# A new order for the first stretch of an RWKV-and-experts kernel: constant products, column turns, stores and loads around the first triangular inversion

## The chip, the cores and the metric

The kernel runs on one core of a Trainium2 chip. The metric is device time in microseconds (us): the median of several executions. One execution was also taken by the hardware profiler. All positions below are microseconds from the start of that execution's span. PE is TensorE, DVE VectorE, ACT ScalarE, POOL GpSimd; SP is the engine that here only issues DMAs.

## What is computed

A recurrence over 768 steps for 4 x 8 heads of width 40, then a dense feed-forward layer, then a layer of eight experts of which each token uses one. The change touches only the recurrence:

```python
for t in range(S):                      # S = 768
    y[:, :, t] = einsum('bhd,bhde->bhe', rt, state)
    Sa = einsum('bhde,bhe->bhd', state, at)
    state = state * wt[:, :, None, :] - einsum('bhd,bhe->bhde', Sa, bt) \
          + einsum('bhd,bhe->bhde', vt, kt)
x = y as 3072 tokens x 320
x = (h * clip(h + 3, 0, 6) / 6) @ w_out          # h = x @ w_in
out[token] = gate * relu(x @ w1[e]) @ w2[e]      # e = argmax expert of the token
```

## The kernel before

The 768 steps are cut into 24 chunks of 32. Within a chunk the recurrence becomes matrix products, for which a unit triangular 32 x 32 system per head and batch must be solved. Two neighbouring chunks are a pair. The steps, with the names that the traces show:

- A **window** is four chunks (128 partitions). `window(sc)` loads `wt`, turns and scans it (`turn`, `scan`, `carry`, `mult`), makes `Em` and its inverse `It` (`before`, `after`, `inv`), scales the rows `ra`, `rk`, `rb` by them (`scale`), and stores what later chunks need to DRAM (`keep`: `Ed`, `KBd`, `X2`, `Pd`). W0 is the first window, W1 the second. Rows 0 to 63 of a window hold its first pair, 64 to 127 its second.
- `prep_u(pair, half)` gives four units: three turn columns (`t`, PE transposes, copied out of PSUM to `Z`, `KB` or `UV`) and the fourth makes the pair's triangular matrices (`LN`, 32 products; masked to `Ns`; stored to `Nd`).
- `solve(pair)` loads `N` (and a copy `X`) from `Nd` and inverts by 30 steps of a product and a subtraction (lines L574, L575). The inverses go to `Td`, and chunks read them back as `Tb`. Pair 0 is solved on DVE, all others on POOL. Each needs its own result only at chunk 2 x pair.
- Chunk c runs, in this order on PE: `rh` (right side), `xp` (turn of the last chunk's output), `u` (product with `Tb`), `tu`, `s` (state), `g` (a triangular product, masked to `YL`), `st`, `y` (output), `vr` (columns of the next chunk). Between them stand units of `prep_u` of a later pair, pieces of the next window, weights of the dense layer (`wraw` loaded, `wf` converted in three DVE operations, `wi`, `wo`), and from chunk 2 on the products of the dense layer itself (`h`, `x`).
- `warmer(n)` and `heat(n)` issue n products of the identity with itself (`warm`), whose result nobody reads. `heat` is called at fixed places of the early chunks, and a table HEATS gives n by the number of the call.

Nothing is scheduled by a machine: each engine works through its instructions in the order in which the program writes them, and waits on semaphores. A DMA queue is in order too: an SP instruction that waits holds all behind it.

Of the kernel before, what the change touches and what calls it, by code (L numbers as in the profile page):

```python
# [42 lines left out]
def kernel(ctx, tc, r, k, v, w, a, b, w_in, w_out, mod_id, w_gate, mod_bias, w1, w2, out):  # L43
# [336 lines left out]
    def init2():  # L380
        nc.vector.tensor_copy(identr, ident)
        nc.scalar.copy(XS[:, 704:768], zeros[:, 0:64])
        nc.scalar.copy(XA[64:104].rearrange("p b h d -> p (b h) d"), ident[64:104, None, 64:104].to_broadcast([40, B * H, D]))

    def window(sc):
# [55 lines left out]
        def keep(j):  # L441

            p, c = slice(C * j, C * j + C), SC * sc + j
            nc.sync.dma_start(out=Ed[c].rearrange("b t f -> t b f"), in_=Em[p].rearrange("p b h e -> p b (h e)"))
            for x in range(2):
                if c == 0:
                    nc.sync.dma_start(out=X2[0][32 * x:32 * x + 32].rearrange("p b h e -> p (b h) e"), in_=AKB[1 + x][p, :, :, 0:D].rearrange("p b h e -> p (b h) e"))
                    continue
                nc.sync.dma_start(out=KBd[x, C * c:C * c + C].rearrange("t b (h e) -> t (b h) e", e=D), in_=AKB[1 + x][p, :, :, 0:D].rearrange("p b h e -> p (b h) e"))
            if j == 0 and sc < NSC - 1:  # L450
                nc.sync.dma_start(out=Pd[sc].rearrange("b f -> (b f)")[None, :], in_=v["I"][127:128].rearrange("p b h e -> p (b h e)"))
# [634 lines left out]
    HEATS = {2: 0, 3: 2, 5: 8, 8: 4, 9: 0, 12: 0, 14: 0, 18: 4, 20: 3, 21: 1, 24: 0, 25: 0, 26: 0, 27: 0, 29: 6, 31: 0, 32: 6, 35: 0, 37: 0, 41: 1, 43: 0, 45: 1, 47: 1, 52: 1, 53: 1, 55: 1, 61: 1, 62: 0, 64: 1, 81: 3, 82: 1, 83: 0}  # L1086
# [13 lines left out]

    def heat(n):

        n = HEATS.get(at[0], 2 if at[0] > 11 else n)
        at[0] += 1
        if n:
            warmer(n)
# [89 lines left out]
    warmer(8)  # L1196
# [3 lines left out]
    keep(0)  # L1200
    keep(1)
    WA.ahead = 0
    WA.pull(1)
    now(wq, 1)
    for kt in range(2):
        nc.sync.dma_start(out=wg[:, kt, :], in_=w_gate[128 * kt:128 * kt + 128, :])
    nc.sync.dma_start(out=wg[0:64, 2, :], in_=w_gate[256:320, :])
    loads_e(0)
    now(U[0][3])
    flush_stores()  # L1210
# [19 lines left out]
    some(2)  # L1230
    now(U[1][3])
    flush_stores()
    some(2)
    work0 = solve(0, nc.vector, None, nc.sync)
    WA.pull(2)
    keep(2)
    keep(3)
    for i in range(3):
        now(U[2][i])
        warmer(2)  # L1240
        now(U[3][i])
# [22 lines left out]
    queue.clear()  # L1264
# [16 lines left out]
    first_units = (2, 2, 1, 2, 1)  # L1281
# [4 lines left out]
    for c in range(NCH):  # L1286
        sc, j = divmod(c, SC)
        more = c + 1 < NCH
        turn = [0]
        if c == SC:  # L1290
            steady.append(True)
            M.lags = (1, 2, 4)
# [4 lines left out]
        def slot(fn, *args):  # L1297
            fn(*args)
            if hold:
                heat(dict(xpose=2, columns=2, turn_state=3, cols_vr=2).get(getattr(fn, "__name__", ""), 0) if c else 0)  # L1300
            tick()

        def dense():
            if (c, turn[0]) >= START and hold:
                hold.pop()
            if len(M.units) > RESERVE and not hold:
                M.emit(1)
            elif c < 4:
                heat(2)
                tick()  # L1310
# [50 lines left out]
        slot(rhs, c)  # L1361
        if c == 0:
            Z.append(big.tile([128, H, B, 2, C], F32, tag="Z2", name="Z2"))
            nc.scalar.copy(Z[2][0:64].rearrange("p h b j t -> p (h b j t)").rearrange("p (n x) -> p n x", x=128), zeros[0:64, None, :].to_broadcast([64, 2 * H, 128]))
            U = [prep_u(2, hf) for hf in range(2)]
            units.extend((U[0][0], U[1][0], *U[0][1:], *U[1][1:]))
# [411 lines left out]
```

## Time and profile before

| | |
|---|---|
| median of 3 runs | 1133.76 us (1129.04 to 1135.96) |
| the profiled execution's own time | 1132.62 us |
| its span | 1130.8 us |
| PE busy | 1038.7 us, 92% of the span |
| DVE, ACT, POOL busy | 675.9, 649.3, 387.5 us |
| granted TensorE clock, mean | 0.922 of full |

The first 230 us are the part in which the chunks run without much of the dense layer between them. After that PE is busy nearly all the time, with the dense layer's and the experts' products.

### The profile page before, as it was taken

The numbers are of one execution on the slowest core, as the hardware profiler recorded it, in microseconds if no ns is written. First come the engines' busy times: TensorE is split into PE (matmuls) and PEld (weight loads), VectorE is DVE, ScalarE is ACT, GpSimd is POOL, SyncE is SP. The second block draws the span as 40 slices with busy tenths as digits, with TensorE's granted clock in tenths as the row PEclk, the third lists the DMA queues.
The fourth block names the chain that finished last, engine by engine and source line by source line (L and its number), as shares of the span: only waits on it lengthen the run. The fifth ranks groups of instructions, "written<-read, shape, count | busy, mean of one in ns | idle before, by whom it ended". The sixth has DMA issues, their size and how long they took to land. (4 is left out here: it accounts for less than half of the span.)

```text
span 1130.8 us, 36970 instructions
## 1 busy us (share of the span) xinstructions
PE 1038.7 (92%) x15598; PEld 969.9 (86%) x15598; DVE 675.9 (60%) x1345; ACT 649.3 (57%) x1364; POOL 387.5 (34%) x844
## 2 busy tenths in 40 slices
PE   3967899899999999998999899999999879999995
PEld 3867898788888887887888798999999879999995
DVE  8676535755546554654335446455666897887770
ACT  4224645578777876777776673433333545666551
POOL 5326260631745738357383701000000102322221
PEclk9566957899999998999999899999999979999998
DMA  9697674997997998779756453133332757666730
GB/s 137 153 107 95 105 153 100 127 174 121 154 140 151 161 128 172 106 142 181 144 106 139 84 131 89 64 104 104 104 91 77 230 166 210 210 200 204 218 92 16
DMA packets 366265, 152.36 MB, mean 135 GB/s; under 512 B 322823, under 2 KB 348935, under 8 KB 366092
## 3 DMA queue, kind: packets, MB, share of 16 engines
q1 hardware_dynamic: 361100, 130.96, 58.9%
q0 software_dynamic: 4992, 18.96, 6.0%
q8 instruction: 125, 2.05, 0.8%
q14 instruction: 48, 0.39, 0.1%
HBM read 109.76 MB, written 40.12 MB: 133 GB/s over the span
## 5 line engine op out<-in xcount | busy, mean ns | idle before, releaser
L275 DVE SCALAR_TENSOR_TENSOR gf<-rl,h 128x512 f32<-128x512 f32 x96 | 65.7, 684 | 128.2 <-ACT rl L271 126.4
L263 PE MATMUL h<-xT,wi 128*128 128x256 f32 x768 | 120.2, 301 | 0.0
L280 DVE TENSOR_TENSOR gl<-gf,gh 128x512 fp32r<-128x512 f32 x78 | 55.3, 709 | 91.9 <-ACT gh L279 91.6
L271 ACT ACTIVATE rl<-h,half 128x512 f32<-128x512 f32 x96 | 66.0, 687 | 73.3 <-PE h L263 72.9
L263 PEld LDWEIGHTS h<-xT,wi 128*128 128x128 f32 x768 | 101.9, 197 | 3.3
L304 PE MATMUL x<-wo,gh 128*128 128x328 f32 x368 | 97.1, 349 | 0.6 <-ACT gh L279 0.6
L1686 POOL DMA_INDIRECT out_dram<-cyo,sidx x26 | 26.2, 1007 | 152.7 <-ACT cyo L1685 130.6
L279 ACT CAST gh<-gf 128x512 fp32r<-128x512 f32 x78 | 48.4, 621 | 39.9 <-DVE gf L275 39.4
L304 PEld LDWEIGHTS x<-wo,gh 128*128 128x128 f32 x368 | 61.8, 198 | 5.2 <-ACT gh L279 0.8
L1096 PE MATMUL warm<-ident 128*128 128x128 f32 x316 | 65.7, 364 | 0.0
L517 ACT COPY Z<-Ns 32x512 f32<-32x512 f32 x48 | 29.6, 617 | 54.5 <-DVE Ns L512 51.1
L1479 POOL DMA_DIRECT2D xTb<-xTd x10 | 5.5, 547 | 161.7 <-PE h L263 161.7
L483 ACT COPY KB<-t 40x512 f32<-40x512 f32 x84 | 48.7, 580 | 19.2 <-PE t L478 17.4
L304 PE MATMUL x<-wo,gl 128*128 128x328 f32 x184 | 59.1, 321 | 0.2 <-DVE gl L280 0.2
L1096 PEld LDWEIGHTS warm<-ident 128*128 128x128 f32 x316 | 54.7, 257 | 3.3
L717 PE MATMUL g<-YL,UV 104*64 104x32 f32 x1536 | 57.5, 230 | 0.0
L717 PEld LDWEIGHTS g<-YL,UV 104*64 104x64 f32 x1536 | 52.0, 145 | 6.1 <-issue 1.5
L506 PEld LDWEIGHTS LN<-Z,KB 104*64 104x64 f32 x1408 | 50.8, 154 | 5.4 <-issue 5.3
L506 PE MATMUL LN<-Z,KB 104*64 104x32 f32 x1408 | 55.1, 236 | 0.0
L1656 ACT ACTIVATE ghc<-ch 128x512 fp32r<-128x512 f32 x35 | 21.0, 599 | 51.3 <-PE ch L1650 50.4
L435 DVE RECIPROCAL It<-It 128x320 f32<-128x320 f32 (+1 forms) x20 | 50.3, 2530 | 0.0
L1570 POOL DMA_INDIRECT xg<-Xr,gidx x26 | 29.7, 1142 | 55.1 <-DVE sidx L1072 21.3
(785 smaller groups left out, 3070.7 us busy)
## 6 DMA issues: line engine op xcount, KB each, us to landing
raw<-in_moe_w_dram SPq DMA_DIRECT2D x26, 512.0 KB
raw<-in_moe_w_dram SPq DMA_DIRECT2D x26, 480.0 KB
xTd<-xT SPq DMA_DIRECT2D x12, 768.0 KB
xTb<-xTd POOLq DMA_DIRECT2D x10, 768.0 KB, 6.6
X<-KBd SPq DMA_DIRECT2D x46, 160.0 KB
raw<-in_moe_w_dram SPq DMA_DIRECT2D x13, 320.0 KB
xpd<-xpart SPq DMA_DIRECT2D x12, 328.0 KB
part<-xpd SPq DMA_DIRECT2D x12, 328.0 KB
```

What stands on the lines that cost most here:

```text
L263: nc.tensor.matmul(hp[:, i, :], lhsT=l, rhs=m, start=j == 0, stop=j == len(seq) - 1)
L271: nc.scalar.activation(v["t"], hv, AF.Relu, bias=half, scale=1.0 / 6.0)
L275: nc.vector.scalar_tensor_tensor(out=v["g"], in0=v["t"], scalar=1.0, in1=hv, op0=ALU.min, op1=ALU.mult)
L279: nc.scalar.copy(gh.rearrange("p i t -> p (i t)"), v["g"])
L280: nc.vector.tensor_tensor(out=gl.rearrange("p i t -> p (i t)"), in0=v["g"], in1=gh.rearrange("p i t -> p (i t)"), op=ALU.subtract)
L304: nc.tensor.matmul(st["x"][tt][:, :NX], lhsT=l[:, i, ts], rhs=W.wo[f][:, m, :], start=fp == 0 and i == 0 and j == 0, stop=fp == NFP - 1 an ...
L435: nc.vector.reciprocal(t, t)
L483: copy(dst[64:104, par::2].rearrange("p g b j t -> p g (b j) t"), pb[HP * par:HP * par + D].rearrange("p g b (j t) -> p g (b j) t", j=2))
L506: nc.tensor.matmul(pv[64 * q:64 * q + 64, g, bb, j, :], lhsT=KB[0:104, h, bb, j].rearrange("p x t -> p (x t)"), rhs=zh[0:104, h, bb, j, :] ...
L717: nc.tensor.matmul(pg[64 * q:64 * q + 64, g, bb, :], lhsT=uv[0:104, h, bb].rearrange("p x t -> p (x t)"), rhs=yl[0:104, h, bb, :], start=T ...
L1096: nc.tensor.matmul(t[:, 0, 0:128], lhsT=ident, rhs=ident, start=True, stop=True)
L1570: nc.gpsimd.indirect_dma_start(out=self.xg[:, i, :], out_offset=None, in_=Xr, in_offset=bass.IndirectOffsetOnAxis(ap=gidx[:, k:k + 1], axi ...
```

## The change

Six things move; no arithmetic of the result changes.

1. In the preparation of the first pair no constant products are left: `warmer(8)` ahead of the first `LN`, the `heat(3)` inside each `LN` and the `warmer(2)` after each column turn of the second pair go. Constant products of chunk 0 are given by the name of the step (HEATS0), later ones by a new HEATS table. The rounded identity is made by ACT, not DVE.
2. The window W1's turn, scan and product stand together ahead of the first inversion, its `after` behind it, its reciprocal in two halves, the second half only after `g` of chunk 0. The first weight conversion stands behind W1's product.
3. `keep(0..3)` (twelve stores and copies) leave after the first inversion's load; the last six from ACT's queue.
4. The next window's rows are loaded in two parts inside the first inversion (`akb_rows`), no longer all behind the load for the second inversion; the inverses' store `Td` follows. The second inversion copies `X` on POOL in place of a second DMA.
5. The zeros of `Z2` are written by POOL, no longer by ACT; the statement stands behind the second inversion in POOL's order.
6. The third pair (2) has its second half, its `k` and `b` columns and both its matrices `LN` turned from chunk 0 to chunks 0 and 1, and pair 3 moves from chunks 1 and 2 to chunks 2 and 3. The inversions 2 and 3 start at the ends of chunks 1 and 3.

```diff
-        nc.vector.tensor_copy(identr, ident)
+        nc.scalar.copy(identr, ident)
...
-    HEATS = {2: 0, 3: 2, 5: 8, 8: 4, 9: 0, 12: 0, 14: 0, 18: 4, 20: 3, 21: 1, 24: 0, ...}
+    HEATS = {2: 0, 4: 0, 8: 1, 10: 0, 12: 1, 14: 1, 19: 1, 20: 1, 22: 1, 28: 1, 29: 0, 31: 1, 48: 3, 49: 1, 50: 0}
...
+    HEATS0 = dict(usolve=4, usolve_cols=2, state=2, wq=2, gram=3, turn_state=2, cols_vr=2)
+    early = [None]
...
-        n = HEATS.get(at[0], 2 if at[0] > 11 else n)
-        at[0] += 1
+        if early:
+            n = HEATS0.get(early[0], 0)
+        else:
+            n = HEATS.get(at[0], 2)
+            at[0] += 1
...
-    warmer(8)
     for i in range(3):
         for h in (h0, h1):
             scale(i, h, nc.gpsimd, pr1)
-    keep(0)
-    keep(1)
...
-    now(wq, 1)
...
-    now(U[0][3])
-    flush_stores()
+    for hf in range(2):
+        now(U[hf][3])
+        flush_stores()
...
-    some(2)
-    now(U[1][3])
-    flush_stores()
-    some(2)
+    both[0] = False
     work0 = solve(0, nc.vector, None, nc.sync)
-    WA.pull(2)
-    keep(2)
-    keep(3)
+    keep(0)
+    keep(1)
     for i in range(3):
         now(U[2][i])
-        warmer(2)
         now(U[3][i])
-        warmer(2)
-    both[0] = False
-    some(1)
+    keep(2, nc.scalar)
+    keep(3, nc.scalar)
+    some(4)
+    now(wq, 1)
+
+    def akb_rows(j):
+        for n in range(6):
+            loads_akb(1, n // 2, j, n % 2)
 
     def next_gram(hf):
+        if not hf:
+            akb_rows(0)
         now(U[2 + hf][3])
         flush_stores()
         if hf:
-            solve(1, nc.gpsimd, None, nc.sync, nc.sync)()()
-
-    def anchor():
+            WA.pull(2)
+            akb_rows(1)
+            solve(1, nc.gpsimd, None, nc.sync)()()
+
+    def before_solved():
+        now(cols_vr, 0)
+        now(rhs, 0)
         warmer(1, work0.X)
-        warmer(24)
-
-    S0, S1, S2 = (2, 7, 15)
-    put0 = work0({S0: lambda: next_gram(0), S1: lambda: next_gram(1), S2: anchor})
-    for n in range(12):
-        loads_akb(1, n // 2 % 3, n // 6, n % 2)
+        warmer(2 * WARM)
+
+    S0, S1, S2 = (6, 10, 20)
+    put0 = work0({S0: lambda: next_gram(0), S1: lambda: next_gram(1), S2: before_solved})
     WA.low = nc.vector
     put0()
-    now(cols_vr, 0)
     loads_t(0)
...
-    first_units = (2, 2, 1, 2, 1)
+    first_units = (0, 1, 1, 1, 1)
...
-            for pr, hf in ([], [(3, 0)], [(3, 1)], [])[c]:
+            for pr, hf in ([], [], [(3, 0)], [(3, 1)])[c]:
...
-            nc.scalar.copy(Z[2][0:64]..., zeros[0:64, None, :].to_broadcast([64, 2 * H, 128]))
+            nc.gpsimd.memset(Z[2][0:64], 0.0)
...
+        if c == 0:
+            half_inverse(1)
...
-        if c == 0:
-            flush_stores()
-            solve(2, nc.gpsimd, None, nc.sync, nc.sync)()()
...
-        if c == 2 or c % 2 and 3 < c < NCH - LEAD - 1:
+        if c % 2 and c < NCH - LEAD - 1:
             flush_stores()
-            solve(3 if c == 2 else (c + LEAD - 1) // 2, nc.gpsimd, None, nc.sync)()()
+            solve((c + LEAD - 1) // 2, nc.gpsimd, None, nc.sync)()()
```

Three places in the engines' orders follow, each before and after. First SP's queue from the grams of pair 1 to the first read of the inverses. `N1None` and `X1None` are loaded for the second inversion, `N0` the first one's result, `ra`, `rk`, `rb` the rows of W1. Before:

```order
L523 DMA Nd_59<-Ns11_650 32x2x256 x2
L565 DMA N1None_656<-Nd_59 64x32x32 x2
L560 DMA X1None_657<-Nd_59 64x16x32 x2
L358 DMA ra_128<-in_a_dram 64x16x40 x2
L358 DMA rk_129<-in_k_dram 64x16x40 x2
L358 DMA rb_130<-in_b_dram 64x16x40 x2
L358 DMA ra_128<-in_a_dram 64x16x40 x2
L358 DMA rk_129<-in_k_dram 64x16x40 x2
L358 DMA rb_130<-in_b_dram 64x16x40 x2
L583 DMA Td_60<-N0_461 1024x1x32 x2
L610 DMA Tb_123<-Td_60 32x8x32 x4
```

After:

```order
L358 DMA ra_128<-in_a_dram 64x16x40 x2
L358 DMA rk_129<-in_k_dram 64x16x40 x2
L358 DMA rb_130<-in_b_dram 64x16x40 x2
L523 DMA Nd_59<-Ns10_565 32x2x256 x2
L523 DMA Nd_59<-Ns11_612 32x2x256 x2
L107 DMA wraw_618<-in_moe_w_in_dram 128x1024
L107 DMA wrawrv_620<-in_moe_w_in_dram 128x1024
L358 DMA ra_128<-in_a_dram 64x16x40 x2
L358 DMA rk_129<-in_k_dram 64x16x40 x2
L358 DMA rb_130<-in_b_dram 64x16x40 x2
L565 DMA N1None_628<-Nd_59 64x32x32 x2
L583 DMA Td_60<-N0_413 1024x1x32 x2
```

The twelve row loads now stand ahead of the second inversion's load, and that stands just ahead of the store of the first inverses.

Second, PE from the right side of chunk 1 to its `u`; `LN20` is the first half of pair 2's matrices. Before (there `LN20` stands in chunk 0, some twenty rows further up, and pair 3's first column turn is here):

```order
L639 MATMUL rh1_1420<-XB_127,Z0_132 32x40 x32
L1096 MATMUL warm_1454<-ident_68 128x128 x2
L761 MATMUL xp0a_1465<-identr_69,XS_143 128x128 x3
L764 MATMUL xp0b_1469<-identr_69,XS_143 128x128 x3
L1096 MATMUL warm_1473<-ident_68 128x128 x2
L478 MATMUL t030_1479<-ident_68,ra_128 104x64 x8
L1096 MATMUL warm_1498<-ident_68 128x128 x2
L649 MATMUL u1_1506<-rh1_1453,Tb_123 32x40 x32
```

After:

```order
L639 MATMUL rh1_1202<-XB_127,Z0_132 32x40 x32
L1096 MATMUL warm_1236<-ident_68 128x128 x2
L761 MATMUL xp0a_1247<-identr_69,XS_143 128x128 x3
L764 MATMUL xp0b_1251<-identr_69,XS_143 128x128 x3
L1096 MATMUL warm_1255<-ident_68 128x128 x2
L506 MATMUL LN20_1261<-Z2_875,KB_126 64x32 x32
L1096 MATMUL warm_1295<-ident_68 128x128 x2
L1096 MATMUL warm_1314<-ident_68 128x128 x2
L649 MATMUL u1_1317<-rh1_1235,Tb_123 32x40 x32
```

`LN20`, which reads all rows of `Z2`, now stands directly ahead of `u` of chunk 1.

Third, POOL at the end of the second inversion. Before:

```order
L574 TENSOR_TENSOR tmp1None_658<-X1None_657,N1None_656 128x15
L575 TENSOR_TENSOR X1None_657<-X1None_657,tmp1None_658 128x15
L578 MEMSET X1None_657 64x16 x2
L583 DMA Td_60<-X1None_657 1024x1x32 x2
L574 TENSOR_TENSOR tmp2None_1289<-X2None_1288,N2None_1287 128x30
L575 TENSOR_TENSOR X2None_1288<-X2None_1288,tmp2None_1289 128x30
```

After:

```order
L574 TENSOR_TENSOR tmp1None_630<-X1None_629,N1None_628 128x15
L575 TENSOR_TENSOR X1None_629<-X1None_629,tmp1None_630 128x15
L578 MEMSET X1None_629 64x16 x2
L583 DMA Td_60<-X1None_629 1024x1x32 x2
L1382 MEMSET Z2_875 64x2048
L562 COPY X2None_1668<-N2None_1667 64x512 x2
```

The zeros of `Z2` come after all of the second inversion and the issue of its two stores.

## Rows read from the trace of the kernel before

**Rows 1.** The page: the span, and the TensorE clock in forty slices of 28.3 us.

```profile
span 1130.8 us, 36970 instructions
...
PEclk9566957899999998999999899999999979999998
```

**Rows 2.** Stretches: start:end, length, each engine's busy time, PEclk, DMA share, GB/s.

```profile
33.00:57.00 24.00, 24.00 (x220) 20.96 (x221) 14.92 (x23) 6.54 (x11) 5.48 (x4) 0.50 0.66 139
39.30:48.40 9.10, 9.10 (x86) 8.02 (x85) 7.51 (x16) 3.62 (x6) 0.00 (x0) 0.50 0.16 36
130.00:165.00 35.00, 31.68 (x435) 28.66 (x435) 13.14 (x26) 14.04 (x33) 25.39 (x64) 0.61 0.87 167
```

**Rows 3.** PE in order of time ahead of the first LN: start, length, [idle before].

```profile
27.95 1.65 PE L478 MATMUL t<-ident,rb 64*104 64x64 f32 x16 [1.38 <-POOL rb L439]
29.53 3.78 PE L1096 MATMUL warm<-ident 128*128 128x128 f32 x16
33.24 1.92 PE L506 MATMUL LN<-Z,KB 104*64 104x32 f32 x32
```

**Rows 4.** DVE in order of time, up to the end of the first inversion.

```profile
25.57 1.56 DVE L381 CAST identr<-ident 128x128 fp32r<-128x128 f32 x1
...
58.55 0.83 DVE L562 COPY N<-N 64x512 f32<-64x512 f32 x2
...
65.10 0.69 DVE L512 TENSOR_TENSOR Ns<-LN,mask 128x512 f32<-128x512 f32 x1 [1.61 <-PE LN L506]
...
81.02 0.22 DVE L578 MEMSET N<- 64x16 f32 x2
```

**Rows 5.** SP's DMA issues in order of time around the inversions.

```profile
68.04 2.17 SPq L565 DMA_DIRECT2D N1None<-Nd  x2
70.25 2.38 SPq L560 DMA_DIRECT2D X1None<-Nd  x2
...
87.32 2.65 SPq L583 DMA_DIRECT2D Td<-N  x2
94.03 1.79 SPq L610 DMA_DIRECT2D Tb<-Td  x4
```

**Rows 6.** Stretches, columns as in rows 2: mixed DMAs, then row loads alone.

```profile
47.00:61.00 14.00, 14.00 (x133) 12.33 (x134) 8.73 (x16) 2.86 (x5) 0.00 (x0) 0.50 0.92 183
77.00:91.00 14.00, 6.08 (x113) 5.66 (x112) 9.18 (x19) 3.36 (x9) 11.73 (x30) 0.72 1.55 134
```

**Rows 7.** POOL in order of time: a memset, the second inversion's ends, a copy.

```profile
0.75 1.81 POOL L1134 MEMSET XB<- 104x2048 f32 x1 [0.29 <-POOLq L1762]
...
76.49 0.24 POOL L574 TENSOR_TENSOR tmp1None<-X1None,N1None 128x30 f32<-128x30 f32 x1 [37.93 <-DMA X1None<-Nd]
...
105.38 0.30 POOL L578 MEMSET X1None<- 64x16 f32 x2
105.81 1.92 POOL L583 DMA_DIRECT2D Td<-X1None  x2
...
204.38 0.60 POOL L562 COPY X3None<-N3None 64x512 f32<-64x512 f32 x1 [40.65 <-DMA N3None<-Nd]
```

**Rows 8.** PE in order of time: from chunk 0 to the end of chunk 1.

```profile
97.22 1.49 PE L649 MATMUL u<-rh,Tb 128*32 128x40 f32 x60 [0.69 <-DMA Tb<-Td]
...
118.70 2.06 PE L506 MATMUL LN<-Z,KB 104*64 104x32 f32 x64
...
129.98 0.80 PE L649 MATMUL u<-rh,Tb 128*32 128x40 f32 x64
...
133.68 1.43 PE L687 MATMUL s<-XA,X 104*40 104x40 f32 x64
...
139.07 1.09 PE L478 MATMUL t<-ident,rb 64*104 64x64 f32 x8 [3.32 <-ACT UV L464]
...
148.75 1.92 PE L506 MATMUL LN<-Z,KB 104*64 104x32 f32 x32
...
162.38 1.30 PE L733 MATMUL y<-X,YL 104*32 104x40 f32 x64
```

More of the change, by code (lines that the diff above doesn't have):

```diff
@@ L439, in scale, with keep @@
             (eng or nc.vector).tensor_tensor(out=t, in0=t, in1=(v["I"] if i else Em)[p, bs, hs], op=ALU.mult)
-        def keep(j):
+        def keep(j, eng=nc.sync):
             p, c = slice(C * j, C * j + C), SC * sc + j
-            nc.sync.dma_start(out=Ed[c].rearrange("b t f -> t b f"), in_=Em[p].rearrange("p b h e -> p b (h e)"))
+            eng.dma_start(out=Ed[c].rearrange("b t f -> t b f"), in_=Em[p].rearrange("p b h e -> p b (h e)"))
             for x in range(2):
@@ L448, in keep @@
                     continue
-                nc.sync.dma_start(out=KBd[x, C * c:C * c + C].rearrange("t b (h e) -> t (b h) e", e=D), in_=AKB[1 + x][p, :, :, 0:D].rearrange("p b h e -> p (b h) e"))
+                eng.dma_start(out=KBd[x, C * c:C * c + C].rearrange("t b (h e) -> t (b h) e", e=D), in_=AKB[1 + x][p, :, :, 0:D].rearrange("p b h e -> p (b h) e"))
             if j == 0 and sc < NSC - 1:
@@ L1085 @@
     RESERVE = 3
-    HEATS = {2: 0, 3: 2, 5: 8, 8: 4, 9: 0, 12: 0, 14: 0, 18: 4, 20: 3, 21: 1, 24: 0, 25: 0, 26: 0, 27: 0, 29: 6, 31: 0, 32: 6, 35: 0, 37: 0, 41: 1, 43: 0, 45: 1, 47: 1, 52: 1, 53: 1, 55: 1, 61: 1, 62: 0, 64: 1, 81: 3, 82: 1, 83: 0}
+    HEATS = {2: 0, 4: 0, 8: 1, 10: 0, 12: 1, 14: 1, 19: 1, 20: 1, 22: 1, 28: 1, 29: 0, 31: 1, 48: 3, 49: 1, 50: 0}
     HEAT = 2
@@ L1199 @@
             scale(i, h, nc.gpsimd, pr1)
-    keep(0)
-    keep(1)
     WA.ahead = 0
     WA.pull(1)
-    now(wq, 1)
[L1205 to L1208, printed above, removed]
-    now(U[0][3])
-    flush_stores()
+    for hf in range(2):
+        now(U[hf][3])
+        flush_stores()
     win = {0: W0, 1: W1}
@@ L1249, in next_gram @@
         if hf:
-            solve(1, nc.gpsimd, None, nc.sync, nc.sync)()()
-    def anchor():
-        warmer(1, work0.X)
-        warmer(24)
-    S0, S1, S2 = (2, 7, 15)
-    put0 = work0({S0: lambda: next_gram(0), S1: lambda: next_gram(1), S2: anchor})
-    for n in range(12):
-        loads_akb(1, n // 2 % 3, n // 6, n % 2)
+            WA.pull(2)
[4 more added lines that the diff above has]
+        now(rhs, 0)
+        warmer(1, work0.X)
+        warmer(2 * WARM)
+    S0, S1, S2 = (6, 10, 20)
+    put0 = work0({S0: lambda: next_gram(0), S1: lambda: next_gram(1), S2: before_solved})
     WA.low = nc.vector
     put0()
-    now(cols_vr, 0)
     loads_t(0)
-    queue.clear()
+    loads_e(0)
+    for kt in range(2):
+        nc.sync.dma_start(out=wg[:, kt, :], in_=w_gate[128 * kt:128 * kt + 128, :])
+    nc.sync.dma_start(out=wg[0:64, 2, :], in_=w_gate[256:320, :])
     load, turn, scan, carry, mult, before, after, inv, scale, keep = W1
@@ L1269, with half_inverse @@
     scale(0, every)
-    for hs in (slice(0, H // 2), slice(H // 2, H)):
+    some(1)
+    queue.clear()
+    def half_inverse(n):
+        hs = slice(n * H // 2, (n + 1) * H // 2)
         inv(every, hs)
@@ L1273 @@
             scale(i, every, hs=hs)
+    half_inverse(0)
     WA.lag, WA.gap = (3, 1)
@@ L1289 @@
         turn = [0]
+        if c == 1:
+            early.clear()
         if c == SC:
@@ L1298, in slot @@
             fn(*args)
+            if early:
+                early[0] = fn.__name__
             if hold:
@@ L1308, in dense @@
             elif c < 4:
+                if early:
+                    early[0] = None
                 heat(2)
@@ L1359, in next_w @@
                     win[sc + 2][0](bb)
-        slot(rhs, c)
+        if c:
+            slot(rhs, c)
         if c == 0:
             Z.append(big.tile([128, H, B, 2, C], F32, tag="Z2", name="Z2"))
-            nc.scalar.copy(Z[2][0:64].rearrange("p h b j t -> p (h b j t)").rearrange("p (n x) -> p n x", x=128), zeros[0:64, None, :].to_broadcast([64, 2 * H, 128]))
+            nc.gpsimd.memset(Z[2][0:64], 0.0)
             U = [prep_u(2, hf) for hf in range(2)]
```

## The prediction

> **What bounds the kernel now.** I read the page first: its line of TensorE's clock has two low places, one from 28 to 113 us and one from 141 to 226 us; elsewhere it stands at 9 tenths [rows 1]. After 230 us PE is full and the change doesn't touch it. So the question is by how much the first stretch becomes shorter. There I read each engine in order of time. Up to 81 us the chain runs through the first inversion on DVE: the matrices `LN` start at 33.24 behind constant products [rows 3], the inversion's copies at 58.55, its end is at 81.2 [rows 4]. Then the inverses wait on SP: DVE is done, but the store `Td` is issued at 87.32, `Tb` is read from 94.03, and `u` of chunk 0 gets its last part at 97.22 [rows 5, 8]. From there the chain is PE's: `u` of chunk 1 starts at 129.98, chunk 1's `y` ends near 163.6, and on the way there is one wait of 3.3 us and a granted clock of 0.61 [rows 2, 8].
>
> **The change, part by part.** All is summed against the profiled execution, 1132.62 us, whose span is 1130.8.
>
> *Up to the first inversion.* The transposes at 27.95 wait for a PSUM bank that a DVE copy frees, behind the rounded identity (1.56 us, [rows 4]): that is 1.4 us, and ACT idles there, so the new place costs nothing. The constant products of 3.78 us [rows 3] and some 7 us of smaller ones go. Then the copies behind the transposes set the start of `LN`, near 29. Both matrices are 32 products each, at the low clock 1.92 us for half of one, so 7.7 us: 36.7. The mask is 0.7: 37.4. Now DVE does W1's work in one piece: 7.51 us busy in its stretch [rows 2] less one mask of 0.69, so 6.8; then a weight conversion of 2 to 4.5 us. The inversion starts near 46 where it started at 58.55. In its 22.7 us two waits for `LN` (the longer 1.61, [rows 4]; the other 0.55) go, because both grams are done before DVE asks. End: 66.5 where it was 81.2. DVE loses half the column copies; ACT takes them, 7 us of work in a stretch where it has 6.5 of 24 us [rows 2].
>
> *SP and the DMA engines.* What follows is not ready at 66.5. The second inversion's load, and right behind it `Td`, stand behind all of `keep` and the row loads. From the first inversion's load (issue near 39.5) to the second's I count 0.5 MB for each of the two loads, 12 stores of 160 KB, 12 row loads of 160 KB, 0.26 MB of `Nd`, and 1.05 MB of weights: 6.2 MB. At 183 GB/s (mixed DMAs [rows 6]) this is 34 us; with the row loads, the `keep` rows and the inversion loads at 134 GB/s, their pace when they alone fill the DMA engines [rows 6], and the rest faster, 38 us. So the second load lands between 73 and 78, I take 77, the slower pace, since small packets are two thirds of the bytes. The `Td` store goes out near 74.5; before, `u` came 9.9 us behind that issue [rows 5, 8], so it comes near 84.5, 13 us earlier than now.
>
> Six of these stores move to ACT's queue. The rows show that one queue alone holds the DMA engines at 1.55, with 134 GB/s [rows 6], so I leave them in the sum. The Trainium skill, "DMA: Bandwidth & Descriptors", section "Issuing engines are not separate DMA queues", has the same: DMAs of SP, ACT and POOL run on the same 16 engines, and another queue saves issue time alone. By it the sum stands; if ACT's queue had a path of its own, 7 us would go from it. On ACT the six issues hold what is behind them: a weight cast, the copies of `Ns`, and chunk 0's columns. No row shows an issue on ACT; the nearest are two on POOL in 1.92 and two on SP in 2.65 [rows 5, 7], so 5.8 to 8 us for six, at 46 to 54. What waits behind is needed only at 84, and costs nothing under that cover.
>
> *The zeros of `Z2`, the new bound.* ACT's copy of 1.9 us goes; POOL's memset takes 1.81 (the like of it, on more partitions [rows 7]). But it stands behind the second inversion. That begins with two copies, 0.6 each [rows 7], at 77, and runs 29.2 us (76.49 to 105.68, [rows 7]), then the two store issues, 1.9, then the memset: 77 + 1.3 + 29.2 + 1.9 + 1.8 = 111.2. `LN20` reads these zeros, and on PE it now stands ahead of `u` of chunk 1, so all of chunk 1 is queued behind this wait. What chunk 0 itself needs (mask of `g`, second half of the reciprocal, output, columns of chunk 1) takes some 21 us from its `u`, so it is ready at 106: five us of the gain on the first inversion are not used. PE idles before `LN20`, so I take it at the low clock: 3.84, then four constant products, 8 x 0.236 = 1.9 and their starts, 2.4 in all: `u` of chunk 1 at 117.5, against 129.98. That is 12.5 us. If the load lands at 70 or at 82, it is 19 or 7.
>
> *Chunk 1.* From its `u` to the end of `s` it takes 5.1 us now (129.98 to 135.04, [rows 8]), at the high clock; after an idle PE I sum the same products, with the new constant ones, to 10.3: 127.8, gain 7.2. From there to the end of `y` now: 28.6 us, of which 3.3 is the wait for ACT, which waits for DVE, which waits for weights that SP issued behind the third inversion's loads. These loads move to the end of the chunk, so this wait goes. 24.6 us are work at the low clock. The same gram takes 2.06 at the high clock and 3.84 at the low one (1.92 for half, [rows 8]), a ratio of 0.54. At the high clock I get 13.3 + 0.7 for two more constant products, 14: end of `y` near 141.8, gain 21.8. At the low clock 25.8: 153.6, gain 10.
>
> Which clock? In chunk 0 now PE starts at 97.22 at the low clock, works without a gap on `u`, constant products, turns and `s`, and the next gram, ten us later, runs at the high one; it holds until the wait of 3.3 us [rows 8]. The new chunk 1 has the same mix behind `LN20` and no such wait, so I take the high clock.
>
> *Later.* Pair 3's second half (three turns of 0.65, a gram of 2.06) comes to stand in chunk 3, which has none now: 4 us on PE if nothing covers it, 0 if chunk 3's waits do, 7.5 at the low clock. I take 4. The inversions 2 and 3 start later, but the later ones already run three chunks ahead in this way; their price is 0 to 3, and I take 0.
>
> *The sum.* 1132.6 - 21.8 + 4 = 1114.8; the median stands 1.1 above this execution, so 1116.
>
> **The rivals.**
> - *The clock stays low through chunk 1.* Between 139 and 163 PE worked without a gap on grams and constant products and stayed at the low clock; from 33 to 57 it was busy 24.00 of 24 us at 0.50 [rows 2, 8]. The new table gives much the same mix. Then 1132.6 - 10 + 4 + 1.1 = 1128. The Trainium skill, "TensorE: Matmul & The Clock Gate", section "What's actually happening", speaks for this one: the throttled state is the default and activity releases it, and the change takes activity away. In the stretch from 33 to 57 the trace says it costs nothing, the clock is at its lower level with the constant products too.
> - *More is freed than I count.* The second load lands at 70 to 73, or the low slices of chunk 2 (0.7 and 0.8 of full from 170 to 226, [rows 1]) go too, worth up to 14 us: with two thirds of that, 1105.
> - *The zeros come too late: slower than before.* One mechanism: the second load behind some 6 MB. At the low clock the gain of 6 us is used up when it lands at 83, and 1% is lost when it lands at 95 or later, which is a pace of 111 GB/s; at 96 the time is 1147. Against it: nowhere in the first 90 us did these DMAs stay at so low a pace while any were waiting.
> - *It does nothing*, 1134, because the first stretch isn't on the path. Against it: PE runs through all chunks in one order, and no load later is tied to the clock on the wall.
>
> **How the numbers follow.** The forecast, high clock in chunk 1, 1109 to 1123: 0.55. Low clock, 1124 to 1131: 0.22. More freed, 1096 to 1108: 0.15. Zeros too late, over 1131: 0.07. Nothing: 0.01. About 1% (11 us) is what a measurement of this kernel can tell. Faster by over that (below 1122.4): nearly all of the first, the third, and a little of the second, 0.70. Within: the rest of the second and a part of the last, 0.24. Slower: 0.06. The range from 1103 to 1130 leaves out the late zeros and half of the third case, some 0.16.
>
> **What the changed profile would show.** DVE's first product of the inversion near 47 and its last memset near 66.5; SP's issue of the second load near 72 with `Td` behind it; `u` of chunk 0 near 84.5; POOL's memset near 109.4 and `LN20` at its end, with PE's longest wait before it, put down to POOL; `u` of chunk 1 near 117.5; `y` of chunk 1 done near 142 with a clock near 1 from 128 on. I am wrong if `LN20` doesn't wait for POOL, if the DMA engines pass the 6.2 MB much faster or slower, or if the clock of chunks 1 and 2 goes another way.

## The result and the profile after

The changed kernel takes 1114.84 us (median of 4 executions, 1112.74 to 1121.23); the kernel before takes 1131.40 (median of 4, of which three had been taken ahead of the prediction; the fourth took 1124.65). The ratio is 0.9898, with a 95% interval of 0.9849 to 0.9948. Measured again (e5 below, 11 and 21 executions) it is 0.9939, 0.9906 to 0.9971. So the change makes the kernel faster by 0.6 to 1.0%, and the two intervals reach from 0.3 to 1.5%. The forecast was 1116, but from a base of 1133.8, a ratio of 0.984; in the sets of the later runs the base alone was 1124 to 1125. The profiled execution of the changed kernel took 1113.57.

The page of the changed kernel, its span and clock in forty slices; against [rows 1] the slice from 139 to 167 us, in which most of chunk 1 lies, stands at 8 tenths where it stood at 5. The slices from 28 to 111 are at 5, 7 and 8 (before 5, 6 and 6), the one from 111 to 139 is at 6 (before 9), and the one from 167 to 195 at 6 (before 7):

```profile
span 1111.8 us, 36869 instructions
...
PEclk9578686999999999998998999999999989999998
```

SP's DMA issues of the changed kernel in order of time; they answer to [rows 5]:

```profile
33.26 4.12 SPq L523 DMA_DIRECT2D Nd<-Ns  x4
44.30 2.92 SPq L565 DMA_DIRECT2D N<-Nd  x2
...
77.04 3.60 SPq L565 DMA_DIRECT2D N1None<-Nd  x2
80.74 2.82 SPq L583 DMA_DIRECT2D Td<-N  x2
86.32 1.83 SPq L610 DMA_DIRECT2D Tb<-Td  x4
...
97.17 0.67 SPq L107 DMA_DIRECT2D wrawxT<-in_moe_w_in_dram  x1
113.20 0.47 SPq L107 DMA_DIRECT2D wrawrv<-in_moe_w_in_dram  x1
...
127.32 0.60 SPq L107 DMA_DIRECT2D wrawxT<-in_moe_w_out_dram  x1
```

What SP waited for longest in 30 to 90 and in 96 to 135 us: who waited, for what, us in total, times, the longest:

```profile
SPq L565 <- DMA Ed<-Em: 6.0, 1, 6.0
...
SPq L107 <- DVE XS L747: 15.8, 1, 15.8
```

The stores of `Ns` for the first inversion are out by 37.4, yet its load leaves at 44.3, where 39.5 was forecast. The wait is put down to a store `Ed`, which ACT issued (line L444, ACT's own queue). Later the queue stands still for 15.8 us at a load of weights into the buffer `wrawrv`, whose last piece DVE has converted only at 113.17 (below). The row names `XS`, the DVE instruction that starts just then; that it is the conversion for which SP waits is shown by e6, which moves it.

DVE, POOL and ACT's queue of the changed kernel in order of time [rows 4, 7]:

```profile
49.42 0.42 DVE L562 COPY N<-N 64x512 f32<-64x512 f32 x1 [4.24 <-DMA N<-Nd]
...
71.27 0.22 DVE L578 MEMSET N<- 64x16 f32 x2
...
112.48 0.69 DVE L118 SCALAR_TENSOR_TENSOR wf<-wrawrv,wf 128x512 int32<-128x512 int32 x1
...
83.32 0.60 POOL L562 COPY X1None<-N1None 64x512 f32<-64x512 f32 x1 [34.03 <-DMA N1None<-Nd]
...
117.51 1.91 POOL L583 DMA_DIRECT2D Td<-X1None  x2
119.46 1.80 POOL L1382 MEMSET Z<- 64x2048 f32 x1
...
42.03 0.37 ACTq L444 DMA_DIRECT2D Ed<-Em  x1
```

PE of the changed kernel in order of time [rows 3, 8]:

```profile
28.23 0.30 PE L506 MATMUL LN<-Z,KB 104*64 104x32 f32 x2 [0.29 <-ACT KB L483]
...
88.22 0.31 PE L649 MATMUL u<-rh,Tb 128*32 128x40 f32 x2 [9.24 <-DMA Tb<-Td]
...
121.31 3.63 PE L506 MATMUL LN<-Z,KB 104*64 104x32 f32 x64 [5.93 <-POOL Z L1382]
...
126.87 1.29 PE L649 MATMUL u<-rh,Tb 128*32 128x40 f32 x64
...
131.36 1.43 PE L687 MATMUL s<-XA,X 104*40 104x40 f32 x64
...
146.43 1.30 PE L733 MATMUL y<-X,YL 104*32 104x40 f32 x64
...
160.23 1.29 PE L649 MATMUL u<-rh,Tb 128*32 128x40 f32 x64
```

`LN20` is the row at 121.31: it waits for POOL's zeros, as forecast, but ten us later than forecast. From `u` of chunk 1 to the end of `y` PE has no wait; the clock of that stretch, columns as in [rows 2], is at 2.4 GHz for most of it (0.93 of full):

```profile
128.00:148.00 20.00, 20.00 (x375) 18.06 (x365) 8.81 (x21) 13.32 (x31) 0.00 (x0) 0.93 0.74 144
```

Starts of the first product of `u` of chunks 0 to 4, and the span, each from PE's rows (line L649) of one profiled execution. With them a reader can see where a run gains and where it gives back. The first column is the kernel; the labels are those of the experiments below. A span is that of one execution and can lie off the median: e3's was the slowest of its ten executions, e12's the fastest of its eleven.

| kernel | u0 | u1 | u2 | u3 | u4 | span |
|---|---|---|---|---|---|---|
| before | 95.97 | 129.98 | 174.50 | 209.37 | 231.03 | 1130.8 |
| before, second profile (e9) | 88.49 | 121.08 | 166.05 | 200.95 | 226.06 | 1127.9 |
| changed | 88.22 | 126.87 | 160.23 | 196.63 | 216.74 | 1111.8 |
| changed, second profile (e5) | 86.06 | 124.27 | 158.68 | 194.68 | 215.16 | 1111.7 |
| e1: zeros on ACT | 88.55 | 121.51 | 159.74 | 195.56 | 216.07 | 1115.6 |
| e2: keep-stores on SP | 86.09 | 124.02 | 159.70 | 196.26 | 216.29 | 1110.8 |
| e3: rows behind Td | 81.09 | 120.02 | 162.09 | 198.33 | 218.86 | 1118.5 |
| e4: no products in chunk 1 | 87.20 | 124.12 | 160.06 | 196.74 | 217.27 | 1119.2 |
| e6: zeros on ACT, conversion early | 88.55 | 120.53 | 155.05 | 190.82 | 211.32 | 1111.8 |
| e7: e6 with e2 and e3 | 77.43 | 122.22 | 160.19 | 196.58 | 216.68 | 1114.7 |
| e8: before, no products in chunk 1 | 89.00 | 120.01 | 166.06 | 196.62 | 225.26 | 1128.4 |
| e10: conversion early alone | 85.59 | 124.50 | 158.43 | 194.96 | 215.28 | 1114.2 |
| e11: e6 with e2 | 85.73 | 117.88 | 153.55 | 190.10 | 210.15 | 1104.8 |
| e12: constant products back | 87.45 | 125.34 | 160.89 | 197.30 | 219.40 | 1113.1 |

### The profile page after: what moved, and what is told of

It reads as the page before. It is cut to its first block, busy times and chain, and to the rows that moved or that the text cites. A ratio compares the mean times of both kernels' runs of the same rounds, so it can differ in the third digit from the quotient of the medians.

```text
span 1111.8 us, 36869 instructions
## 1 busy us (share of the span) xinstructions
PE 1009.5 (91%) x15540; PEld 944.4 (85%) x15540; DVE 666.6 (60%) x1338; ACT 650.1 (58%) x1370; POOL 392.3 (35%) x849
## 5 line engine op out<-in xcount | busy, mean ns | idle before, releaser
L1673 ACT ACTIVATE ghc<-ch 128x512 fp32r<-128x512 f32 x35 | 20.9, 598 | 51.0 <-PE ch L1667 50.0
L724 DVE TENSOR_TENSOR YL<-g,mask 64x512 f32<-64x512 f32 x48 | 32.9, 685 | 20.3 <-PE g L717 19.9
L1096 PE MATMUL warm<-ident 128*128 128x128 f32 x258 | 44.5, 324 | 0.0
```

What stands on the lines that cost most here:

```text
L724: nc.vector.tensor_tensor(out=yl[0:64, par::2], in0=pg[q:q + 64], in1=mask[q:q + 64, None, None, :].to_broadcast([64, 4, B, C]), op=ALU.mult)
L1096: nc.tensor.matmul(t[:, 0, 0:128], lhsT=ident, rhs=ident, start=True, stop=True)
```

## The experiments

My theory after the result: the chain of the forecast holds, and three places delay it, the load at 44.3, the zeros behind the second inversion, and SP's queue. The rivals: the clock gives back what starts earlier, or something else ends at the same time. A ratio is always to the kernel before in the same set of executions. In the expectations of e7, e8, e9 and e12 the places of the high or low clock are counted from a zero some 10 us ahead of the span's start; in what follows them, from the span's start.

**e1: the zeros back on ACT.**

```diff
-            nc.gpsimd.memset(Z[2][0:64], 0.0)
+            nc.scalar.copy(Z[2][0:64]..., zeros[0:64, None, :].to_broadcast([64, 2 * H, 128]))
```

> The changed kernel with one part undone: the zeros of Z2 are written by ScalarE again, ahead of its copy of u of chunk 0, and no more by GpSimd behind the second inversion. Theory (the zeros are the last wait ahead of LN20): LN20 starts at about 115.4 in place of 121.3, when the matmuls in front of it end, and u of chunk 1 at about 121 in place of 126.9; the time falls by some 6 us to about 1109. Rival (something else ends there at the same time, or the later chunks give it back): the wait ahead of LN20 is put down to another releaser at 119 or later, and the time stays within 2 us of 1115.

1117.45 us (10 executions), ratio 0.9943 (0.9904 to 0.9982). PE, DVE and SP of this run:

```profile
115.94 3.63 PE L506 MATMUL LN<-Z,KB 104*64 104x32 f32 x64 [0.41 <-ACT YL L619]
...
140.76 1.55 PE L169 MATMUL wg<-wg,wtT 128*128 128x8 f32 x6 [1.95 <-DVE Ns L512]
...
140.01 0.69 DVE L512 TENSOR_TENSOR Ns<-LN,mask 128x512 f32<-128x512 f32 x1 [5.32 <-DMA Nd<-Ns]
...
137.12 4.39 SPq L523 DMA_DIRECT2D Nd<-Ns  x4
```

The zeros were the last wait ahead of `LN20`: it starts at 115.94, and u1 at 121.51. But u2 stays at 159.7, and the time falls by nothing that shows, where 6 us had been expected. The place is the DVE row: the second mask `Ns` waits 5.32 us for the store of the first, which SP issues only at 137.12 (136.29 in the changed kernel): SP's queue doesn't move with PE.

**e2: the keep-stores of rows 64 to 127 on SP.**

```diff
-    keep(2, nc.scalar)
-    keep(3, nc.scalar)
+    keep(2)
+    keep(3)
```

> The changed kernel with one part undone: the six keep-stores of rows 64 to 127 are issued on SyncE's queue again (behind the first inversion's load) and no more on ScalarE's. Theory (the first inversion's load waits, through a completion semaphore that it shares with ScalarE's first store, for that store, which ScalarE issues only at 42.0): the load goes out at 39.5 to 40.5 in place of 44.3, the first product starts near 48.5 in place of 53.0, the first inversion ends near 67, and if the bytes in front of the second load are what times that, it too comes some 4 us earlier; time about 1110 to 1111. Rival 1 (the load waits for the stores of Ns to land, or for VectorE): it stays at 43 to 44.3 and the time at 1115. Rival 2 (the six issues on SyncE's queue, 4.8 us, put the second load back by as much as the first comes forward): u of chunk 0 is 4 us earlier, LN20 stays near 121, time 1115.

1116.86 us, ratio 0.9945 (0.9913 to 0.9977). SP, DVE and PE of this run:

```profile
38.85 2.03 SPq L565 DMA_DIRECT2D N<-Nd  x2
...
74.17 3.72 SPq L565 DMA_DIRECT2D N1None<-Nd  x2
...
65.30 0.22 DVE L578 MEMSET N<- 64x16 f32 x2
...
118.45 3.63 PE L506 MATMUL LN<-Z,KB 104*64 104x32 f32 x64 [6.82 <-POOL Z L1382]
```

The load leaves at 38.85, 5.45 us earlier than in the changed kernel, and the first inversion ends at 65.5, where 66.5 had been forecast. So the load did wait for ACT's store. The list of semaphores on which the changed program's instructions wait says how. SP's first load, then ACT's first store:

```
L565 DMA N0_413<-Nd_59 64x32x32 [waits DMAHW4_49,DMAHW5_49,DMAHW3_49,DMAHW6_49,DMAHW0_49,DVE_49]
L444 DMA Ed_58<-Em_117 32x4x320 [waits DMAHW0_49]
```

Each DMA of SP or ACT signals its end on one of eight semaphores, which the program gives out in turn to both queues. The four stores of `Ns` hold numbers 3 to 6. Number 0 was last given to ACT's store, so the load must wait until that has landed, and ACT issues it at 42.03, among its column copies. The store thus goes out ahead of the load that it was to follow. With the stores on SP the load shares none with ACT. What this is worth is little: the second load comes at 74.17 (77.04 in the first profile of the changed kernel, 74.34 in the second), u0 at 86.09 (88.22 and 86.06), `LN20` at 118.45 (121.31 and 118.70). So the second rival is right that the stores then fill SP's queue, but u0 has not the 4 us that it gave.

**e3: the rows of the second half behind Td.**

```diff
             WA.pull(2)
-            akb_rows(1)
             solve(1, nc.gpsimd, None, nc.sync)()()
...
     put0()
     loads_t(0)
+    akb_rows(1)
```

> The changed kernel with one move: the loads of rows 64 to 127 of the second window stand behind the second inversion's load and the first inversion's Td store and Tb loads on SyncE's queue, in place of ahead of them. Theory (those six loads hold the queue from 67.5 to 77.0, and both the second load and Td stand behind them): second load at about 67.5, Td at about 72, u of chunk 0 at about 80 in place of 88.2, the second inversion and the zeros of Z2 about 8 us earlier, LN20 at 111 to 113, time 1105 to 1107. Rival (the rows are needed as soon as they come: the columns of ra in front of the state of chunk 0 wait for them, so that chunk 0 ends no earlier): the wait ahead of the columns t of ra grows by as much as u gains, LN20 gains at most 2 to 3 us, time 1112 to 1115.

1115.91 us, ratio 0.9917 (0.9887 to 0.9946). PE in order of time, then the stretch after it:

```profile
89.53 1.09 PE L478 MATMUL t<-ident,ra 64*104 64x64 f32 x8 [4.16 <-DVE ra L439]
```

```profile
90.00:105.00 15.00, 15.00 (x185) 13.62 (x183) 14.01 (x14) 5.64 (x11) 12.89 (x28) 0.50 0.61 107
```

u0 comes at 81.09, seven us earlier, but the columns of `ra` then wait 4.16 us for rows that come late, and from 90 to 105 PE works without a gap at 1.2 GHz (0.85 of full in the changed kernel). u1 is at 120.02, u2 at 162. `LN20` starts at 116.94, where the theory had 111 to 113. Theory and rival share it: the first gain is real, and the rows and the clock take most of it back.

**e4: no constant products in chunk 1.** The calls of `heat` do nothing while c is 1.

> The changed kernel without the constant products (warmers) of chunk 1 alone; their results are used nowhere. Theory (in chunk 1 they keep TensorE's clock at its high level; u of chunk 1 to u of chunk 2 takes 33.4 us there against 44.5 before): the granted clock of chunk 1 falls to 1.2 GHz for most of it, the stretch from u1 to u2 grows to 38 to 45 us and the time to 1119 to 1126. Rival (the clock was high for another reason, such as the matmuls that fill the chunk's waits, and the warmers only cost): u1 to u2 stays at 31 to 34 us and the time at 1113 to 1116.

1118.53 us, ratio 0.9945 (0.9907 to 0.9982). The stretch of chunk 1:

```profile
120.00:160.00 40.00, 38.10 (x567) 34.06 (x567) 17.59 (x40) 22.18 (x57) 9.23 (x23) 0.50 0.80 152
```

The clock falls to 1.2 GHz for all of the chunk, as my theory had it, but most of the cost isn't there: from u1 to u2 it takes 35.9 us, below the theory's 38 to 45 (33.4 with the products, 34.4 in the second profile, 35.6 and 35.7 in e12 and e2, which leave chunk 1 as it is), and from u1 to the end of `y` 22.1 against 20.9. So the clock in chunk 1 is worth at most 3 us net of the products that keep it up, not 11.8.

**e5: the changed kernel again**, beside e6 to e8.

> The changed kernel as it is, on the chip of the next three runs, as what they are compared with. Every theory: a ratio of 0.985 to 0.995 to the kernel before.

1117.31 us, ratio 0.9939 (0.9906 to 0.9971).

**e6: the zeros on ACT and one conversion earlier.** As e1, and with it:

```diff
-    convert = {(0, 3): 2, (0, 5): 1, (0, 6): 1,
+    convert = {(0, 1): 1, (0, 3): 2, (0, 6): 1,
```

> The changed kernel with the zeros of Z2 on ScalarE (as in the first experiment), and one conversion of a piece of weights moved from the fifth dense place of chunk 0 to the first, so that the buffer wrawrv is converted ahead of the mask of g of chunk 0. Theory (in the first three experiments u of chunk 2 stayed at 160 to 162 though u of chunk 1 was 3 to 7 us earlier, since SyncE's queue stands from 98 to 113 at the load into wrawrv, whose buffer VectorE frees at 113, and the stores of Ns20 and the weights of chunk 1 are queued behind it): the queue passes wrawrv at 97 to 101, the stores of Ns20 leave at about 121 in place of 137, Ns21 does not wait for them, no wait of TensorE for weights of over 1 us stands in chunk 1, u of chunk 2 at about 154 and the time some 5 us below the changed kernel. Rival (the low clock takes it back, or chunk 2 is set by something else, such as the second inversion): u of chunk 2 stays at 158 to 162, the time that of the changed kernel within 2 us.

1111.13 us, ratio 0.9870 (0.9829 to 0.9911). SP and PE:

```profile
99.33 0.47 SPq L107 DMA_DIRECT2D wrawrv<-in_moe_w_in_dram  x1
...
129.09 1.07 SPq L523 DMA_DIRECT2D Nd<-Ns  x1
...
114.96 3.63 PE L506 MATMUL LN<-Z,KB 104*64 104x32 f32 x64
...
148.76 0.76 PE L158 MATMUL wt<-ident,wf 128*128 128x128 f32 x3 [1.67 <-DVE wf L118]
```

SP passes `wrawrv` at 99.3 in place of 113.2 (and then waits 8.1 us for the right side of chunk 1 to free `XB`, which I had not seen coming: the stores of `Ns20` leave at 129, not 121, and one wait of PE for weights stays, 1.67 us). u2 comes at 155.05, 4.7 us earlier than with the zeros alone.

**e7: all four edits**, those of e6, e2 and e3.

> The changed kernel with all four edits: the zeros on ScalarE, the six keep-stores on SyncE's queue, the rows 64 to 127 of the second window behind Td, and the conversion of wrawrv earlier. Theory (the queue of SyncE is what holds chunks 0 and 1): u of chunk 0 at 77 to 80, u of chunk 1 at 112 to 117, u of chunk 2 at 147 to 152, time 8 to 12 us below the changed kernel, about 1103 to 1107. Rival (the clock: what starts earlier runs at 1.2 GHz, as chunk 0 did from 99 to 126 with the rows behind Td): u of chunk 1 at 117 to 120, u of chunk 2 at 156 to 162, time within 3 us of the changed kernel.

1115.63 us, ratio 0.9896 (0.9849 to 0.9942). The rival's case: u0 at 77.43, the earliest of all, and u1 at 122.22 behind waits of 1.9 and 7.0 us ahead of the columns of `ra`, and with the clock at 0.50 of full from 78 to 118. u1 is even later than the rival's 117 to 120. Without the edit of e3 this kernel is e11, with u2 at 153.55 for 160.19 here.

**e8: the kernel before without constant products in chunk 1.**

> The kernel before without the constant products of chunk 1 (their results are used nowhere). There, u of chunk 1 to u of chunk 2 took 44.5 us, of which the clock was at its low level from 148 to 175; the changed kernel without them in chunk 1 ran all of chunk 1 at the low clock in 35.9 us. Theory (at the low clock the constant products cost more than they bring: they stand between the chunk's own products): u1 to u2 falls to 36 to 40 us and the time by 4 to 8 us against the kernel before. Rival (they keep the clock up for the first half of the chunk, and without them the chunk's own products take twice as long): u1 to u2 stays at 43 to 48 us, time the same or up to 4 us more.

1131.14 us, ratio 1.0052 (1.0018 to 1.0085). From u1 to u2 it takes 46.0 us: the rival's size, but only in part for its reason. DVE and SP in order of time, then the stretch of the chunk:

```profile
127.08 0.44 DVE L116 TENSOR_SCALAR wf<-wrawrv 64x512 int32<-64x512 int32 x1 [5.09 <-DMA wrawrv<-in_moe_w_in_dram]
...
141.74 0.47 DVE L116 TENSOR_SCALAR wf<-wrawxT 128x320 int32<-128x320 int32 x1 [9.65 <-DMA wrawxT<-in_moe_w_out_dram]
...
121.09 2.15 SPq L107 DMA_DIRECT2D wrawrv<-in_moe_w_in_dram  x1
...
135.56 1.48 SPq L107 DMA_DIRECT2D wrawxT<-in_moe_w_out_dram  x1
```

```profile
120.00:166.00 46.00, 32.93 (x507) 29.06 (x505) 19.86 (x43) 23.06 (x58) 25.77 (x64) 0.59 0.91 162
```

PE idles 13 of 46 us, where in e4, without these products and at a lower clock, it idled 1.9 of 40. DVE waits 14.7 us for two pieces of weights, and ACT's casts and column copies wait behind DVE. SP issued these pieces at 121.09 and 135.56, after it had stood 9.4 us at the stores of pair 2's `Ns` and had issued the third inversion's four loads at 116.80 to 121.04. The change moves those to the end of the chunk. In the first profile of before, PE idles only 3.3 us from u1 to u2: there the constant products are busy for 18.5 us (3.1 here), and stand in what would else be waits. The rival's part is that the chunk's other products are busy for some 30 us here and some 23 there. The median is 0.5% longer than before, clear of the noise; up to u4 the profiles of e8 and e9 are alike, so where this is lost stays open.

**e9: the kernel before, a second profile.**

> The kernel before as it is, for a second profile of it. In the run of the kernel before without the constant products of chunk 1, all that stands ahead of chunk 1 is the same as before, and yet u of chunk 0 came at 89.0 there against 95.97, with the clock at its high level from 43.4 to 57.1. Theory (the stretch ahead of chunk 0 of the kernel before has executions of two kinds, by the clock that its constant products and columns get there): u of chunk 0 at about 89 or at about 96, and where it is 89, the clock was high for over 10 us between 40 and 60; span 1115 to 1125 in the first case, 1127 to 1132 in the second. Rival (u of chunk 0 at 95.97 is what the kernel before always does): 95 to 97.

Its time is 1128.17 us, a ratio of 1.0001 (0.9951 to 1.0052). Its profiled execution has u0 at 88.49, and the clock from 33 to 57 at 0.73, where [rows 2] has 0.50; until 44 it is 0.99:

```profile
33.00:57.00 24.00, 20.61 (x294) 18.52 (x294) 20.54 (x40) 7.49 (x13) 5.36 (x4) 0.73 0.84 166
```

So the stretch ahead of chunk 0 has executions of both kinds, and u0 was as early as my theory had it. The span of 1127.9 is not as short as the theory had it, nor is that of e8.

**e10: the earlier conversion alone** (the diff of e6 without that of e1).

> The changed kernel with the earlier conversion of wrawrv alone (the zeros stay on GpSimd, behind the second inversion). Theory (two gates in a row, the zeros ahead of u of chunk 1 and SyncE's queue ahead of u of chunk 2; opening one alone is worth little): u of chunk 1 stays at 124 to 127, SyncE's queue passes wrawrv by 101, u of chunk 2 at 157 to 160, the time that of the changed kernel within 2 us, a ratio of 0.992 to 0.994. Rival (all of the gain of the version with both comes from the conversion): u of chunk 2 at about 155, a ratio near 0.987.

1115.66 us, ratio 0.9931 (0.9904 to 0.9959); u1 at 124.50, u2 at 158.43. SP passes `wrawrv` at 96.25 and nothing comes of it: two gates in a row, as expected.

**e11: e6 with the keep-stores on SP.**

> The changed kernel with three edits: the zeros on ScalarE, the earlier conversion, and the keep-stores of rows 64 to 127 on SyncE's queue; the rows of the second window stay ahead of Td. Theory (with both gates open, what the first inversion gains by going out at 39 reaches the end): u of chunk 0 at 85 to 86, u of chunk 1 at 117 to 118, u of chunk 2 at 151 to 153, a ratio of 0.984 to 0.985, 2 to 3 us below the version with two edits. Rival (the clock of chunk 0 or 1 falls and takes it): u of chunk 2 at 154 to 158, a ratio of 0.987 to 0.990.

1106.60 us (5 executions, 1104.63 to 1109.07), ratio 0.9850 (0.9805 to 0.9895), the fastest of all. PE:

```profile
112.31 3.63 PE L506 MATMUL LN<-Z,KB 104*64 104x32 f32 x64
...
117.88 1.24 PE L649 MATMUL u<-rh,Tb 128*32 128x40 f32 x64
```

`LN20` has no wait, u1 is at 117.88, u2 at 153.55. Its interval lies below that of the changed kernel's second measurement; it overlaps those of e6 and of the first measurement, so what the stores on SP add to e6 isn't told apart.

**e12: the constant products of the first stretch back.**

```diff
         now(U[1][i])
+    warmer(8)
     for i in range(3):
...
         now(U[2][i])
+        warmer(2)
         now(U[3][i])
+        warmer(2)
```

> The changed kernel with the constant products of the first stretch put back, one part of the change undone: eight ahead of LN00, and two behind each of the six groups of columns of the second pair. Theory (on the way to the first inversion's load they only delay it, 3.7 us for the eight in the profile before): LN00 at 32 in place of 28.2, the first inversion's load at 47 to 49, u of chunk 0 at 90 to 93, time 2 to 4 us above the changed kernel, a ratio of 0.996 to 0.998. Rival (they raise the clock between 40 and 60, as it was seen once in the kernel before, and the columns and LN behind them run in half the time): u of chunk 0 at 86 to 88, a ratio of 0.992 to 0.995.

1118.54 us, ratio 0.9961 (0.9936 to 0.9986). PE in order of time, then a stretch behind it:

```profile
30.18 2.06 PE L506 MATMUL LN<-Z,KB 104*64 104x32 f32 x64
```

```profile
40.00:45.00 5.00, 4.62 (x115) 4.12 (x115) 3.36 (x6) 3.18 (x6) 0.00 (x0) 1.00 0.56 91
```

Both sides are half right. `LN00` starts 2 us later, but runs whole in 2.06 at 2.4 GHz; the clock is high until 50, and the load leaves at 43.2 (44.3 and 42.5 in the two profiles of the changed kernel). The load's time alone says little, since here too it waits 6.1 us for ACT's store `Ed`; but ahead of that wait the stores of `Ns` are out by 36.2 (37.4 and 35.6). u0 is at 87.45. So leaving the constant products out of this stretch saves nothing on the way to the first inversion that one profile can show, and this one is of the fastest execution. Over eleven executions each, the granted clock of the whole kernel is 0.942 in the median here and 0.936 in e5, yet the time is no shorter: the ratios (0.9961 here, 0.9939 and 0.9898 without) overlap in their intervals.

## Why the prediction was right where it was, and where it wasn't

The time fell into the range, and the mechanism that it names as the new bound is the one in the trace. That it fell so near is in part luck: the terms of its sum were not of the sizes given, and they offset each other. At the end of `y` of chunk 1 the gain was to be 21.8 us and was 16.0 (163.7 against 147.7). Behind it 4 us were to be lost; 1.7 were lost up to u4, and 4.7 came back in the part of which the prediction says that the change doesn't touch it. So 17.8 stand against 19.0, in one execution each. As a ratio, 0.984 was forecast, and 0.9898 and 0.9939 were measured.

- *Up to the first inversion* (forecast 66.5, measured 71.5). `LN` and W1's work came as summed (28.2 and 43.4 for 29 and 44.2). The step that failed is that ACT's issues cost nothing under their cover: the cover was looked for on ACT, and the price arose on SP, 5.45 us, by a semaphore that both queues share (e2). With it undone the end is 65.5.
- *6.2 MB from the first load to the second.* From 44.3 it took until 77.0 for the issue and 83.3 for the landing, 39 us, where I had taken 37.5. The start was late and the pace near, 157 GB/s; but the working was wrong. By its own terms, 4.9 MB at 134 GB/s and 1.3 MB at 183 take 44 us, not 38, so that the true pace lies between the two. In e2 the second load is issued at 74 though the first leaves at 38.9. With the six stores on ACT's queue the DMA engines moved 157 GB/s from the first load's issue to the second's landing, with all on SP's 151 (e2): the second queue gave little or no bandwidth. The Trainium skill, "DMA: Bandwidth & Descriptors", section "Issuing engines are not separate DMA queues", says that DMAs run on the same 16 DMA engines whichever engine issues them; these two numbers agree.
- *The zeros of `Z2`, the new bound.* Right in kind (121.31, [5.93 <-POOL]); ten us later than 111.2, six of them from the late load, two from the second inversion (31.4 us from its first product to its last memset, for 29.2) and one from its copies. u1 gained 3.1 us, not 12.5. Against the second profile of before it even came later, 124 to 127 for 121.
- *Chunk 1.* The high clock was right, its price wrong. I had put 3.3 us on the wait that goes with the third inversion's loads and 11.8 on the clock; the two sizes are nearly the other way round. At a low clock (0.50 and 0.59) and nearly without constant products, u1 to u2 takes 35.9 us with the change (e4) and 46.0 without it (e8), and PE's idle time makes the difference: 1.9 us of 40 against 13.1 of 46. Not all of this is the loads' new place. Against e8 the two pieces of weights are issued 7.9 and 8.2 us earlier (113.20 and 127.32), but chunk 1 also starts 6.9 us later, behind the zeros. Where u1 comes as early as in the second profile of before (e1, 121.51 for 121.08), u1 to u2 takes 38.2 us against 45.0, so the gain is 6.7 us and not 11. That the loads' place and not another part of the change brings it is read from the traces; a kernel with that part alone was not tried.
- *Later: 4 us for chunk 3.* Wrong: from u3 to u4 it takes 20.1 and 20.5 us in the changed kernel, 21.7 and 25.1 in the two profiles of before and 28.6 in e8. Pair 3's units came to stand where PE had waited ahead of the turn of the state (1.9, 2.7 and 6.2 us, put down to DVE `XB`); in the changed kernel that wait is gone.
- The price of 0 for the later start of the inversions 2 and 3 held but for one wait of PE for `Tb`, 0.8 us at chunk 5 (0.9 in the second profile).

From u4 to the end the changed kernel gains some 5 us more (14.3 grows to 19.0 between the first profiles, 10.9 to 16.2 between the second). Of it some 2.5 are waits of PE for `Tb` between 250 and 680 us (5.4 and 5.2 us before, 2.9 and 2.8 after); what sets these was not tried, and stays open, as does the clock's share of the rest. PE's wait in chunk 3 of before, and the waits for `Tb` before and after:

```profile
221.02 1.96 PE L705 MATMUL st<-ident,XB 40*104 40x40 f32 x16 [1.88 <-DVE XB L680]
```

```profile
PE u L649 <- DMA Tb<-Td: 5.4, 4, 2.0
...
PE u L649 <- DMA Tb<-Td: 2.9, 2, 2.7
```

Of the rivals, "the clock stays low" came in e4, where the products had gone with it, and cost at most 3 us. "More is freed" did not come: the second load landed later, and from 170 to 226 us the clock is 0.82 (0.79 before). e11 frees more, at other places. "The zeros come too late" was the nearest miss: the load landed at 83.3, the point from which it was to lose time at the low clock; the freed waits of chunk 1 paid for it.

## What to carry to other kernels

When a DMA moves to another engine's queue, list which completion semaphores it shares with DMAs on the critical path, and when that engine will come to issue it: a store that nobody needs yet can hold a load on another queue until it has landed (6.0 us here). Opening one gate of two in a row shows nothing in the time (e1, e10), so look at the next landmark before dropping the edit; both together brought 1117.31 to 1111.13 in one set of executions (e5, e6), with intervals that overlap by a hair. And price a low clock with and without the products that are there to prevent it.

## What the runs showed of the hardware that I had not expected

The same program gets different clocks in different executions. The kernel before had 0.50 of full from 33 to 57 us in the profiled execution of [rows 2], and 0.73 in another (e9), and u0 came 7.5 us earlier there, with the same instructions; e8, which is the same up to chunk 1, has u0 at 89.0. How much of the 7.5 us is the clock's isn't shown. The Trainium skill, "TensorE: Matmul & The Clock Gate", section "What's actually happening", says that the number of slow matmuls at a kernel's start differs between runs of one kernel; the traces agree, with more than that at stake here. In the changed kernel and all its variants but e12 the clock from 33 to 57 is 0.50, ten profiles out of ten. Where the constant products that the change takes away are in place, it is higher in three of four (0.87 in e12, 0.73 in e9, 0.78 in e8; 0.50 in the first profile of before). So they can raise it and don't always, and e12 shows no gain in time. The first point of the change says that none are left in the preparation of the first pair; 48 of them, from 18 to 26 us, stand in both kernels, and in both the clock is at 2.4 GHz at their end.

A second thing is the queue that isn't the engine's own: the load on SP waited 6.0 us, to 44.30, for a DMA of ACT's queue, which ACT issued only at 42.03. What tied them is the semaphore that the program gave to both.
